# A planner that begins a pair of score tiles when its second PSUM bank is still being emptied

## The chip, the cores and the metric

The kernel runs on one core of a Trainium2 chip. The core has a matrix engine (TensorE, PE in the profile, with its weight loads shown as PEld), a ScalarE (ACT), a VectorE (DVE), a GpSimd (POOL), and a queue for transfers on SyncE (SP). PE writes into PSUM, which this kernel uses as eight banks of 128 partitions by 512 float32; the other engines read PSUM and work in SBUF. The metric is the device time of one execution in microseconds, the median of several.

## What is computed

Two layers, each made of a multi-query attention block and a mixer with an MLP, over 2048 tokens of width 512. The attention has 32 query heads of 16 elements, and all heads share one key head and one value head:

```
def _A_ref(x, wq, wk, wv, wo):              # x is the layer-normed input
    q = (x @ wq).reshape(B, S, H, Dh)...    # H = 32, Dh = 16
    k = x @ wk                              # one head for all
    v = x @ wv
    scores = einsum("bhqd,bkd->bhqk", q, k) * (Dh ** -0.5)
    p = softmax(scores)
    o = einsum("bhqk,bkd->bhqd", p, v)
    return o.reshape(B, S, H * Dh) @ wo
def _B_ref(x, w1, w2, w3, w4):
    h = gelu(layernorm(x) @ w1)             # 512 -> 512
    ...                                     # four column groups shifted by +1, -1, +2, -2 tokens
    hs = shifted @ w2
    x1 = x + hs
    return x1 + gelu(layernorm(x1) @ w3) @ w4   # 512 -> 1792 -> 512
x = x + _A_ref(layernorm(x)); x = x + _B_ref(layernorm(x))   # twice
```

The scores are 32 x 2048 x 2048 per layer, and each needs an exponential. That is the bulk of the work.

## The kernel before

**The plan.** The Python program declares operations (`Plan.op`, each with an engine, a guessed duration, a priority and the data that it reads and writes), and a list scheduler (`Plan.run`, `_pick`, `_place`) places them in simulated time, engine by engine. A lower priority number goes first. The order that comes out is written down for each engine by `emit`, with semaphore waits. So the planner's guesses decide the order; on the chip each engine then works through its own list in that order, and waits where it must. The guess for an eviction of 512 columns from PSUM by VectorE is `t_ps(512)`, 0.600 us, and 0.085 us more until the bank counts as free.

**The halves.** The attention is cut into 2,048 pieces that the code calls halves: for one chunk of queries (512 tokens, in the last two chunks of layer 1 256), one block of 4 heads, one tile of 128 keys (two for the small chunks), and one pair of heads (`p` is 0 or 1). A half is 128 x 1024 scores in two PSUM banks. Its matmuls (`qk`, line 973) contract over 32 rows, so a half uses two of the four groups of 32 rows of the matrix engine, and a half with the other `p` can run beside it.

A half is worked on in one of two ways:

- As a **unit** (`declare_unit`): two matmuls fill two of the four banks set aside for ScalarE, ScalarE takes the exponential of all 1024 columns in one instruction (line 1017, tile EA), and one group of matmuls adds the product with the values (VP) to the accumulator bank (line 1096, one half of it).
- As a **pair** (`declare_pair`): two matmuls fill two banks of a common pool, each one a tile of the pair. VectorE turns each tile into integers whose bits are an approximate bfloat16 exponential (line 1038, tile J, one instruction for each tile). GpSimd then writes two shifted copies (line 1048, tile JK), and three groups of matmuls add J and the two JK, each with its own scaled values (VD). When four of the copies are already waiting on GpSimd, a copy is planned for VectorE. There are three J buffers and four JK buffers.

Every half that goes to a pair is one that ScalarE does not have to do.

**The pool.** Banks 5, 6 and 7 are the pool. The pair tiles use them, and so does all side work: projections, transposes, output projection, mixer and MLP, each as a matmul tile that VectorE evicts. Side work has priority 10 in the main part, units 0, pair tiles 0.5, VectorE's J 1 and the product matmuls 2. When an evicting operation is placed, its bank is entered in the pool with the planned time at which it comes free. `_pick` gives a waiting tile a bank when that time plus 0.06 us (pair tiles) or 0.15 us (side work) has come. A pair tile that can't start beside a unit's score matmuls is put behind nearly everything (`deferred`, priority 11).

**When a pair begins.** Each time the score matmuls of a unit are placed, `attach` looks at the pool: with at least `FREE` = 2 banks free it calls `assign`, so that both tiles can run in the row groups that the unit leaves unused. `assign` still refuses when `MAX_PAIRS` = 2 earlier pairs are unfinished on VectorE, when the side work that is ready on VectorE comes to more than `BACKLOG` = 1 us, when a product is held back too long, or when no half with the right `p` has its data. Two stretches have stricter limits (`CALM`, `CALM_END`). If nothing was assigned for `LONELY` = 3 us, `pump` calls `assign` whatever the pool holds.

**The order of the whole.** Layer 0 has four chunks and layer 1 five. The side work of one chunk is spread (`PACE`) over the attention of the next. After the last chunk of each layer the chain output projection, mixer, MLP is urgent. At the change of layers the first chunk of layer 1 works on the keys that are there already. `filler` matmuls (ONES, NIL) fill idle time on PE to keep its clock up.

Of the kernel before, what the change touches and what calls it, by code (L numbers as in the profile page):

```python
# [15 lines left out]
class Late:  # L16
# [4 lines left out]
    def __init__(self):  # L21
        self.bank = None
        self.ops = []
        self.gates = []
# [481 lines left out]
class Kernel:  # L506
# [29 lines left out]
    FAR = 20  # L536
    FREE = 2
    LONELY = 3

    def __init__(self, nc, ins, out):  # L540
        self.nc = nc
# [651 lines left out]
    def pump(self, now):  # L1193
# [3 lines left out]
        while True:  # L1197
# [9 lines left out]
            did = True  # L1207
        if now > self.attached + self.LONELY and self.assign(now, self.ndve % 2):
            did = True
# [8 lines left out]

    def attach(self, q):

        if sum(1 for t, b in self.pl.pool if t + 0.06 <= self.pl.now) >= self.FREE:
            self.assign(self.pl.now, 1 - q.pe[3][0] // 2)

    def assign(self, now, p):
# [276 lines left out]
```

The softmax here doesn't subtract the row's maximum and nothing guards it: scores larger than these inputs give would overflow.

## Time and profile before

| | |
|---|---|
| median of 5 runs | 1599.46 us (1597.3 to 1600.16) |
| the profiled execution | 1599.78 us, of which its span is 1597.7 us |
| granted PE clock, mean | 0.998 |
| ACT busy | 1506.4 us (94%) |
| DVE busy | 1214.8 us (76%) |
| POOL busy | 1133.1 us (71%) |
| units (EA, line 1017) | 1,509 instructions, 1397.5 us |
| pair tiles (J, line 1038) | 1,078 instructions, so 539 pairs, 698.9 us |
| copies (JK, line 1048) | 955 on POOL, 123 on DVE |

The span runs from the first to the last instruction; 2.1 us lie around it. Busy shares are averages over stages that differ. The attention ends near 1540 us, and the last 58 us are the tail of the last chunk. A group of the profile's list shows the line, the engine, the operation, output and inputs, the count, then busy time, mean duration of one, and the engine's idle time just before such instructions with what ended it. Neighbouring instructions of one engine overlap a little, so busy time over count (926 ns for a unit) is less than the mean duration (1088 ns).

### The profile page before, as it was taken

To read this page: it belongs to the slowest core of one execution; us is meant where nothing else is said; L and a number is where in the kernel's file an instruction comes from. 1 tells how busy PE (TensorE), PEld (TensorE's weight loads), DVE (VectorE), ACT (ScalarE), POOL (GpSimd) and SP (SyncE) were. 2 spreads that over 40 slices of the span, in tenths; PEclk is the share of its full clock that TensorE was granted. 3 is DMA by queue.
4 is the path that set the end of the run, shared out by engine and by line. 5 is a ranking of instruction groups with operands and counts; after the bars stand their busy time and mean duration, and the time that the engine had idled before them with its cause. 6 is when DMAs were issued, how large, how long until landed. Compare 5 with 4: busy or idle time off the path is not lost.

```text
span 1597.7 us, 63318 instructions
## 1 busy us (share of the span) xinstructions
PE 1554.0 (97%) x28709; PEld 648.0 (41%) x28709; DVE 1214.8 (76%) x2145; ACT 1506.4 (94%) x1585; POOL 1133.1 (71%) x1149
## 2 busy tenths in 40 slices
PE   8999999999999999999999999999999999999999
PEld 3333333433333334343333534334433333554445
DVE  8777878877887668887785577878687876888863
ACT  4999999999999999999999779999999999999972
POOL 4799887688886557867575367787887776678640
PEclk9999999999999999999999999999999999999999
DMA  6100010001000001000000000100000000000000
GB/s 209 17 6 5 6 18 6 4 4 21 6 5 4 5 5 19 6 4 2 2 2 2 3 7 11 19 4 4 15 13 5 6 4 14 18 8 8 6 10 25
DMA packets 32142, 21.51 MB, mean 13 GB/s; under 512 B 12673, under 2 KB 31361, under 8 KB 31873
## 3 DMA queue, kind: packets, MB, share of 16 engines
q1 hardware_dynamic: 31872, 17.47, 4.6%
q8 instruction: 224, 3.67, 0.9%
q14 instruction: 46, 0.37, 0.1%
HBM read 7.90 MB, written 2.10 MB: 6 GB/s over the span
## 4 chain that ended last, share of the span: by engine, by line
ACT 74%; PE 23%; DVE 2%; issue 0%; DMA 0%; POOL 0%; SPq 0%; POOLq 0%
ACT EA L1017 69%; PE PB L625 9%; PE PB L973 7%; PE PB L1096 5%; ACT G L1428 2%; ACT L1017 1%; PE PB L791 1%; ACT GP L1348 1%; ACT L1428 1%; ACT L1348 0%; DVE G L1421 0%; DVE ST L736 0%; DVE J L1038 0%; PE PB L834 0%; PE PB L901 0%
## 5 line engine op out<-in xcount | busy, mean ns | idle before, releaser
L1017 ACT ACTIVATE EA<-PB 128x1024 bf16<-128x1024 f32 x1509 | 1397.5, 1088 | 47.3 <-PE PB L973 37.7
L1048 POOL TENSOR_SCALAR JK<-J 128x1024 uint16<-128x1024 uint16 x955 | 1009.0, 1057 | 354.9 <-DVE J L1038 228.9
L1038 DVE TENSOR_SCALAR J<-PB 128x512 uint16<-128x512 f32 x1078 | 698.9, 683 | 195.8 <-PE PB L973 191.6
L973 PE MATMUL PB<-QT,KT 32*128 32x512 bf16 (+1 forms) x4608 | 623.8, 360 | 26.0 <-ACT EA L1017 15.0
L1096 PE MATMUL PB<-EA,VP 128*32 128x256 bf16 (+1 forms) x6796 | 385.3, 264 | 0.9 <-DVE QT L1108 0.5
L973 PEld LDWEIGHTS PB<-QT,KT 32*128 32x128 bf16 x4608 | 160.4, 91 | 434.9 <-ACT EA L1017 314.1
L1096 PE MATMUL PB<-JK,VD 128*32 128x256 bf16 (+1 forms) x4840 | 288.6, 265 | 2.9 <-POOL JK L1048 1.9
L1096 PEld LDWEIGHTS PB<-EA,VP 128*32 128x32 bf16 x6796 | 159.0, 95 | 159.1 <-issue 128.5
L625 PE MATMUL PB<-ZT,W 128*32 128x512 bf16 (+2 forms) x2816 | 170.4, 342 | 0.2
L1096 PEld LDWEIGHTS PB<-JK,VD 128*32 128x32 bf16 x4840 | 114.3, 95 | 135.3 <-issue 83.7
L625 PE MATMUL PB<-ONES,NIL 128*32 128x512 bf16 x1764 | 154.3, 390 | 6.3 <-DVE ZR L773 2.0
L1096 PE MATMUL PB<-J,VD 128*32 128x256 bf16 (+1 forms) x2420 | 153.3, 263 | 1.4 <-DVE J L1038 0.6
L625 PE MATMUL PB<-W,G 128*32 128x512 bf16 x1624 | 114.4, 383 | 1.1 <-ACT G L1428 1.1
L1421 DVE CAST G<-PB 128x512 bf16<-128x512 f32 (+2 forms) x126 | 73.0, 583 | 31.7 <-PE PB L625 31.2
L1048 DVE TENSOR_SCALAR JK<-J 128x1024 uint16<-128x1024 uint16 x123 | 80.8, 664 | 4.9 <-PE PB L1096 3.6
L625 PEld LDWEIGHTS PB<-ZT,W 128*32 128x32 bf16 x2816 | 63.8, 96 | 32.5 <-issue 18.6
L1096 PEld LDWEIGHTS PB<-J,VD 128*32 128x32 bf16 x2420 | 59.8, 95 | 37.1 <-issue 22.7
L625 PEld LDWEIGHTS PB<-ONES,NIL 128*32 128x32 bf16 x1764 | 43.9, 96 | 41.9 <-issue 10.5
L1428 ACT ACTIVATE G<-G 128x3584 bf16<-128x3584 bf16 (+2 forms) x18 | 46.0, 2601 | 14.9 <-DVE G L1421 14.8
L1157 DVE TENSOR_TENSOR OS<-ACCF,PB 128x512 bf16<-128x512 bf16 (+1 forms) x72 | 44.8, 622 | 17.0 <-PE PB L1151 16.9
L756 POOL TENSOR_TENSOR SM<-SM,MH 128x4 f32<-128x4 f32 (+3 forms) x39 | 37.0, 950 | 22.4 <-DVE SM L758 19.6
L625 PEld LDWEIGHTS PB<-W,G 128*32 128x32 bf16 x1624 | 37.3, 96 | 29.7 <-issue 13.8
(94 smaller groups left out, 873.8 us busy)
## 6 DMA issues: line engine op xcount, KB each, us to landing
OT<-OS SPq DMA_DIRECT2D x424, 8.0 KB, 1.8
W<-in_B_w_dram SPq DMA_DIRECT2D x2, 1792.0 KB, 14.7
QT<-QS SPq DMA_DIRECT2D x40, 64.0 KB, 2.5
X<-in_A_x_dram SPq DMA_DIRECT2D x8, 256.0 KB, 5.1
out_dram<-OUTB SPq DMA_DIRECT2D x16, 128.0 KB, 1.7
OT<-OS SPq DMA_DIRECT2D x104, 4.0 KB, 1.8
W<-in_B_w_dram SPq DMA_DIRECT2D x2, 512.0 KB, 8.2
WQ<-in_A_wq_dram SPq DMA_DIRECT2D x1, 512.0 KB, 4.4
```

The lines of the kernel that those rows point to most:

```text
L625: ins = e.matmul(self.PB[32 * g:32 * g + 32, bank, 0:n], lhsT=lhsT[:, 32 * g:32 * g + 32], rhs=rhs, start=start, stop=stop, tile_position= ...
L756: op("POOL", lambda e: e.tensor_tensor(out=out, in0=src, in1=self.MH[:, 0, a:b], op=ALU.pow), reads=tags + [("MH",)], writes=tg(r), dur=0. ...
L791: ins = e.transpose(self.PBH[:, L.bank, j * 512 + i * 128:j * 512 + (i + 1) * 128], rows[:, tb % 4, dc * 128:(dc + 1) * 128], self.IDENT)
L973: ins = e.matmul(self.PB[:, bank, j * n:(j + 1) * n], lhsT=self.KT[32 * h:32 * h + 32, la, (kb + j) * 128:(kb + j + 1) * 128], rhs=self.QT ...
L1017: o = q.feeds = op("ACT", lambda e: e.activation(self.EA[:, ea, :, :], self.PB[:, b0:b0 + 2, :], ACTF.Exp, scale=0.25), writes=bk + [("EA" ...
L1038: o = op("DVE", lambda e, i=i, L=L: e.tensor_scalar(out=J[:, i * 512:(i + 1) * 512], in0=self.PB[:, L.bank, :], scalar1=128 * LOG2E * 0.25 ...
L1048: x = op(eng, lambda e, k=k, r=r: e.tensor_scalar(out=self.JK[:, r, :], in0=J, scalar1=float(self.STEPS[k]), scalar2=1.0, op0=ALU.add, op1 ...
L1096: ins = e.matmul(self.PB[32 * x:32 * x + 32, self.ACC, p * hw:p * hw + hw], lhsT=v[:, la, kb + j, :], rhs=ap[:, i, j * w + u * hw:j * w + ...
L1157: op("DVE", lambda e: e.tensor_tensor(out=self.OS[:, m, 0:n], in0=acc, in1=self.PB[:, M.bank, 0:n], op=ALU.mult), reads=[("ACCF", m)], wri ...
L1348: return e.activation(self.GP[:, par, :, 2:2 + n], self.GP[:, par, :, 2:2 + n], ACTF.Gelu_apprx_tanh)
L1421: op("DVE", lambda e, f=f, L=L: e.tensor_copy(self.G2[:, f, 0:n], self.PB[:, L.bank, 0:n]), writes=[L, ("G2", f)], dur=t_ps(n), give=L)
L1428: ins = e.activation(self.G2[:, a:a + 7, 0:n], self.G2[:, a:a + 7, 0:n], ACTF.Gelu_apprx_tanh)
```

## The change

A constant is added, and the test in `attach` counts a bank as available when its planned time of coming free (plus 0.06 us) lies within the next 0.45 us, not only when it is past. Nothing else is changed; the rules by which a tile gets its bank and the tests in `assign` are as they were. The order of all later work is planned anew with it.

```
@@ class Kernel
     FREE = 2
     LONELY = 3
+    SOON = 0.45
...
     def attach(self, q):
-        if sum(1 for t, b in self.pl.pool if t + 0.06 <= self.pl.now) >= self.FREE:
+        if sum(1 for t, b in self.pl.pool if t + 0.06 <= self.pl.now + self.SOON) >= self.FREE:
             self.assign(self.pl.now, 1 - q.pe[3][0] // 2)
```

More of the change, by code (lines that the diff above doesn't have):

```diff
@@ L538 @@
     LONELY = 3
+    SOON = 0.45
     def __init__(self, nc, ins, out):
@@ L1219, in attach @@
     def attach(self, q):
-        if sum(1 for t, b in self.pl.pool if t + 0.06 <= self.pl.now) >= self.FREE:
+        if sum(1 for t, b in self.pl.pool if t + 0.06 <= self.pl.now + self.SOON) >= self.FREE:
             self.assign(self.pl.now, 1 - q.pe[3][0] // 2)
```

## The prediction

> **What bounds the kernel now.** I read the page's engine sums and its chain first, then the costliest groups, then who waits for whom, then the timeline of a quiet stretch and of one with side work.
>
> ```profile
> PE 1554.0 (97%) x28709; PEld 648.0 (41%) x28709; DVE 1214.8 (76%) x2145; ACT 1506.4 (94%) x1585; POOL 1133.1 (71%) x1149
> ...
> ACT 74%; PE 23%; DVE 2%; issue 0%; DMA 0%; POOL 0%; SPq 0%; POOLq 0%
> ...
> L1017 ACT ACTIVATE EA<-PB 128x1024 bf16<-128x1024 f32 x1509 | 1397.5, 1088 | 47.3 <-PE PB L973 37.7
> L1048 POOL TENSOR_SCALAR JK<-J 128x1024 uint16<-128x1024 uint16 x955 | 1009.0, 1057 | 354.9 <-DVE J L1038 228.9
> L1038 DVE TENSOR_SCALAR J<-PB 128x512 uint16<-128x512 f32 x1078 | 698.9, 683 | 195.8 <-PE PB L973 191.6
> ...
> L1048 DVE TENSOR_SCALAR JK<-J 128x1024 uint16<-128x1024 uint16 x123 | 80.8, 664 | 4.9 <-PE PB L1096 3.6
> ```
>
> ScalarE is the bound: 74% of the chain, and before its 1,509 exponentials only 47.3 us idle. One costs 1397.5 / 1509 = 0.926 us, so a half moved from a unit to a pair is worth 0.926 us while ACT has no gaps. The takers are not full: VectorE waited 191.6 us for score matmuls ahead of a J, and POOL 228.9 us for a J.
>
> ```profile
> PEld PB L973 <- ACT EA L1017: 314.1, 895, 2.2
> ...
> POOL JK L1048 <- DVE J L1038: 228.9, 197, 8.7
> DVE J L1038 <- PE PB L973: 191.6, 241, 6.8
> ```
>
> These are waits: total, number, longest. The first says that ahead of 895 of the score groups PE stood 314.1 / 895 = 0.35 us waiting for ScalarE to empty a unit's banks. That slack covers small delays on PE.
>
> The timeline near 121 us, no side work:
>
> ```profile
> 121.04 0.39 PE L973 MATMUL PB<-QT,KT 32*128 32x512 bf16 x4
> ...
> 121.51 1.29 DVE L1038 TENSOR_SCALAR J<-PB 128x512 uint16<-128x512 f32 x2 [0.55 <-PE PB L973]
> ...
> 121.96 0.39 PE L973 MATMUL PB<-QT,KT 32*128 32x512 bf16 x2
> ...
> 122.83 0.43 DVE L1048 TENSOR_SCALAR JK<-J 128x1024 uint16<-128x1024 uint16 x1
> 122.88 0.39 PE L973 MATMUL PB<-QT,KT 32*128 32x512 bf16 x4
> ```
>
> x4 is a unit and a pair together, x2 a unit alone. Both take 0.39 us: a pair that joins a unit is free on PE. It joins every second unit, at 121.04 and 122.88, so the cadence is 1.84 us. At 121.96 two banks are being emptied: the first J of the pair began at 121.51, and of the two evictions in 1.29 us it ends near 122.16, 0.20 us after that group starts. The third bank is free. One is free and one is soon: the old test says no, the new one yes.
>
> **The change part by part.**
>
> *How often the answer changes.* For 1,336 units up to 1,365 us I rebuilt from the trace's instructions which of the three pool banks were held (a bank is held from the first matmul of its tile to the end of the eviction that reads it). At 510 units score tiles of a pair were issued too, at 826 none. Of these 826, 228 had two or more banks free already, so the other tests refused; 199 had none free; 157 had one free and no other within 0.39 us (0.45 less the 0.06 in the test); 242 had one free and another coming within 0.39 us. The change speaks to the 242: 57 of them between 50 and 200 us, where the quiet cadence rules, the others at some 8 in 50 us. Scaled to 1,509 units: 242 x 1509 / 1336 = 273. Where two banks were free, 395 of 395 + 228 units went with a pair, 63%; so some 172 pairs will be begun at a moment at which none was before. Most are not additional ones: they take the place of the pair that the next unit would have begun.
>
> *How many are additional.* That is set by the time that VectorE has left. A pair costs it two evictions of 1.29 / 2 = 0.645 us and, when POOL is full, two copies. POOL is nearly full in the quiet stretch (126 instructions busy 133.6 of 150 us between 50 and 200 us), so I charge both copies to VectorE at the mean of its 123, 0.664 us: 1.29 + 1.33 = 2.62 us. The 191.6 us of waiting would then hold 73 pairs, the upper end. I take the share of it that this test guards: of the 598 units refused for want of banks (242 + 157 + 199) the change opens 242, 40.5%. 0.405 x 191.6 / 2.62 = 30 pairs. The lower end is 0: MAX_PAIRS and the backlog test stay, and may hand the same count at other times. I take 30, since the quiet stretch, where the count of openings is thickest, shows the cover: 0.55 us of DVE waiting in each 2 x 1.84 us.
>
> *What they save.* 30 x 0.926 = 27.8 us of ScalarE. The product matmuls of a pair are three groups where a unit has one, some 0.11 us apart in the timeline: 0.22 us more PE for each half moved, 6.6 us in all, hidden beside ScalarE in the 0.35 us per group and in the fillers (154.3 us of ONES matmuls, which the planner leaves out when there is work). If that cover were gone, 6.6 us would come back.
>
> *What is late next.* The second tile of an early pair is no longer free on PE. It can join only a unit with the other pair of heads, or runs by itself. The side-work stretch near 306 us shows a group where one tile went ahead of the unit and could not share:
>
> ```profile
> 305.55 0.39 PE L973 MATMUL PB<-QT,KT 32*128 32x512 bf16 x3
> ...
> 306.10 0.60 PE L973 MATMUL PB<-QT,KT 32*128 32x512 bf16 x3
> ```
>
> 0.60 against 0.39: a lone tile costs 0.21 us. 172 x 0.21 = 36 us if all go alone and nothing hides them, 0 if all join. Behind it in PE's order stand products and the next unit's scores, and ScalarE waits for the latter; 0.21 is inside the 0.35 us of slack, so I cost it at nothing in most stretches. It has no cover where ACT is not the bound: from 800 to 960 us ACT is busy 138.5 of 160 us. I found 21 openings between 800 and 950 us, x 0.63 = 13 pairs; a side tile put off by a bank loses one eviction, 0.69 us (mean of the 512-column G evictions), at most 9 us. I take 4, half, rounded; the ends are 0 and 9. The queues of SP and POOL get nothing new: POOL's copies follow their J as before. The tail after 1540 us holds no pairs and stays, 58 us.
>
> *A rule weighed.* VectorE's copies had durations of 380 / 500 / 1402 ns (minimum, median, maximum), POOL's 1047 median; the longest is about one POOL copy, 1.05, and a free one, 0.38, end to end. The Trainium skill's page "SBUF — State Buffer", section "SBUF: two separate sides", says that VectorE in its two-port modes and GpSimd take the port pair that they share as an exclusive lock for a whole instruction. By the rule at its worst each extra copy takes 1.43 us, a pair 4.15, and the sum would be 0.405 x 191.6 / 4.15 = 19 pairs, 17 us, instead of 28; it speaks against the change, since a fuller POOL locks more often. The trace agrees with the maximum, the median says that it is mostly less.
>
> *Sum.* 1599.8 (this execution) - 27.8 + 4 = 1576. The execution lies 0.3 us above the median of 1599.46, which is nothing here. About 0.2%, 3 us, is what a measurement of this kernel can tell from no change.
>
> **The rivals.**
>
> *A, more pairs, as above: 1576.* Own range 1545 to 1594.
>
> *B, the same count, begun earlier: 1599, within 3 us.* For it: POOL at 89% between 50 and 200 us, and the 228 units at which two banks were free and nothing was begun, so banks are not the only limit. Against: 191.6 us of VectorE waiting, 228.9 us of POOL waiting.
>
> *C, slower: PE stalls in order on the second bank.* The order is written with guessed durations: an eviction 0.600 us, the trace 0.645 to 0.69; a copy on VectorE is guessed at 0.33 us and takes 0.664. A fuller VectorE runs behind the plan, and the second tile then stands at PE's head until the eviction ends, with the next unit's scores behind it. Price: up to 0.39 us of wait and 0.21 us alone, less the 0.35 of slack, 0.25 us of ScalarE's time for each of 172 pairs, 43 us; with 28 gained, +15, 1615. It decides from 28 / 172 = 0.16 us lost per early pair on. For it: between 750 and 800 us there is no filler at all, so PE has no room there. Against: in that same window ACT is busy 49.97 of 50 us, and PE now waits on a J ahead of scores only 3.5 us in the whole span. The Trainium skill's page "TensorE: Matmul & The Clock Gate", section "The mechanism" under "Part 3: Packing small matmuls — row/col tiling", says that matmuls start and end strictly in program order, which would make C's stall hit all that follows; no row here shows one overtaking.
>
> *D, all of the waiting is filled: 73 pairs, 68 us, 1532.* For it: copies took only 0.43 us in the quiet stretch. Against: only 40.5% of the bank refusals are opened.
>
> **How the numbers follow.** A 0.46, B 0.09, C 0.37, D 0.08. A is always faster, so is D; of B I count 0.07 as the same and 0.01 on each side; C is slower, up to its full price. Faster 0.55, same 0.07, slower 0.38. The range leaves out most of D below and the worst of C above: 1545 to 1617.
>
> **What would show it.** Right: about 570 pairs for 539, units near 1,480 for 1,509, VectorE's wait for scores well below 191.6 us, more groups of x3 and fewer of x2, ACT's idle before EA near 47 us. B: pairs within 5 of 539. C: pairs up or level, but ACT's idle before EA risen by tens of us with PE named as the releaser, and PE's wait ahead of L973 for a J far above 3.5 us. The prediction fails if side work, which shares the three banks, is put off so far that the stretch from 800 to 960 us or the tail grows by more than 24 us.

## The result and the profile after

| | before | after |
|---|---|---|
| median | 1599.46 us | 1595.68 us |
| ratio | | 0.9986 (95% interval 0.9981 to 0.9991) |
| the profiled execution / its span | 1599.78 / 1597.7 us | 1597.41 / 1595.6 us |
| pairs / units | 539 / 1,509 | 559 / 1,489 |
| ACT busy / idle in the span | 1506.4 / 91.3 us | 1488.2 / 107.4 us |

The kernel became faster by 0.14%: less than the 0.2% that was set as the bound of "no change", though the interval lies wholly below 1. The ratio is close to that of the means over all executions (1598.75 and 1596.47 us, 2.3 us apart); the medians are 3.8 us, 0.24%, apart. ScalarE was relieved of 18.2 us, and stood idle for 16.1 us more. That is the whole case: where did the new idle time come from?

The page of the kernel after (one line has been added above the functions, so each line number is higher by one): the engine sums, the chain, and the costliest groups.

```profile
PE 1552.6 (97%) x28725; PEld 660.2 (41%) x28725; DVE 1273.9 (80%) x2258; ACT 1488.2 (93%) x1563; POOL 1101.1 (69%) x1116
...
PE 51%; ACT 42%; DVE 6%; issue 1%; POOL 0%; DMA 0%; SPq 0%
...
L1018 ACT ACTIVATE EA<-PB 128x1024 bf16<-128x1024 f32 x1489 | 1382.1, 1069 | 46.4 <-PE PB L974 29.3
L1049 POOL TENSOR_SCALAR JK<-J 128x1024 uint16<-128x1024 uint16 x922 | 977.7, 1060 | 387.6 <-DVE J L1039 236.9
L1039 DVE TENSOR_SCALAR J<-PB 128x512 uint16<-128x512 f32 x1118 | 723.0, 682 | 156.2 <-PE PB L974 151.7
...
L1049 DVE TENSOR_SCALAR JK<-J 128x1024 uint16<-128x1024 uint16 x196 | 131.6, 678 | 12.3 <-PE PB L1097 11.1
...
L1429 ACT ACTIVATE G<-G 128x3584 bf16<-128x3584 bf16 (+2 forms) x18 | 46.0, 2601 | 31.7 <-DVE G L1422 31.6
```

Twenty more pairs, twenty units fewer, and VectorE's wait for scores is down from 191.6 to 151.7 us. The idle time ahead of the exponentials is 46.4 us, as good as the 47.3 of before. Whoever looks at that group alone finds nothing lost. The loss stands in the last line: a Gelu of the MLP, which has only 18 instructions and takes 46.0 us in both kernels, now has 31.7 us of idle time before it, where it was 14.9. The chain has changed hands too, PE leads it with 51%: a path followed back through a gap of ScalarE runs on the engine that filled the gap.

What ScalarE waits for, by line, before:

```profile
ACT EA L1017 <- PE PB L973: 37.7, 11, 18.4
ACT G L1428 <- DVE G L1421: 14.8, 1, 14.8
ACT EA L1017 <- PE PB L1096: 8.8, 3, 6.2
```

and after (total, number, longest):

```profile
ACT G L1429 <- DVE G L1422: 31.6, 2, 17.6
ACT EA L1018 <- PE PB L974: 29.3, 17, 18.6
ACT EA L1018 <- PE PB L1097: 14.9, 4, 5.6
```

The Gelu's second wait is in the tail of both kernels (14.8 and 14.0 us), the one of 17.6 is new. Gelu waits rise by 16.8 us and waits for product matmuls (L1097) by 6.1; waits for scores fall by 8.4.

To see where, I cut both executions into stages, each ended by a certain copy of the accumulator of the attention (the 32nd ends the attention of layer 0, the 47th the stretch that I call the change of layers). All columns are us, worked out from the instructions of the two traces.

| stage | length before | after | ACT idle before | after |
|---|---|---|---|---|
| attention of layer 0 | 758.1 | 739.9 | 26.6 | 24.9 |
| change of layers | 177.6 | 187.5 | 21.6 | 28.6 |
| layer 1, rest of the 512-token chunks | 419.1 | 413.6 | 0.3 | 0.8 |
| layer 1, first 256-token chunk | 91.5 | 102.4 | 0.2 | 9.7 |
| layer 1, second 256-token chunk | 92.3 | 94.0 | 0.1 | 1.4 |
| tail | 59.1 | 58.3 | 42.6 | 41.9 |

The windows view gives the same for three of these stages (window, length, busy us of PE, PEld, DVE, ACT, POOL with counts, granted clock, DMA share, GB/s). Before:

```profile
0.00:758.10 758.10, 735.06 (x12397) 288.33 (x12397) 596.96 (x1043) 731.53 (x771) 574.47 (x577) 1.00 0.08 19
758.10:935.70 177.60, 171.80 (x2920) 71.29 (x2916) 121.19 (x230) 156.05 (x160) 94.12 (x101) 1.00 0.01 2
1354.90:1446.40 91.50, 89.97 (x2566) 46.81 (x2566) 75.90 (x141) 91.35 (x97) 64.21 (x67) 1.00 0.06 13
```

After:

```profile
0.00:739.90 739.90, 719.21 (x12121) 287.80 (x12121) 619.54 (x1085) 715.00 (x758) 552.27 (x553) 1.00 0.08 19
739.90:927.40 187.50, 181.40 (x3150) 77.88 (x3146) 135.44 (x257) 158.86 (x159) 99.44 (x106) 1.00 0.01 2
1341.00:1443.40 102.40, 98.82 (x2686) 50.20 (x2682) 76.52 (x144) 92.73 (x98) 67.58 (x71) 0.98 0.06 14
```

Length less ACT busy is the idle time: 177.60 - 156.05 = 21.6 against 28.6; 91.50 - 91.35 = 0.2 against 9.7. The attention of layer 0 is 18.2 us shorter, 8.8 of them because a Gelu of the third chunk's MLP, which ran at 736 us, now runs at 790, in the next stage. Then two places give back: the change of layers 9.9 us, most of it that Gelu, and the first small chunk 10.9.

The change of layers, ScalarE's own timeline (start, length, instruction, the idle time before it). Before:

```profile
894.85 12.26 ACT L1017 ACTIVATE EA<-PB 128x1024 bf16<-128x1024 f32 x13 [6.24 <-PE PB L1096]
927.73 12.94 ACT L1017 ACTIVATE EA<-PB 128x1024 bf16<-128x1024 f32 x14 [14.73 <-PE PB L973]
```

After:

```profile
800.73 11.80 ACT L1018 ACTIVATE EA<-PB 128x1024 bf16<-128x1024 f32 x12 [1.27 <-PE PB L974]
812.55 1.28 ACT L1429 ACT_TABLE_LOAD   x1
831.47 4.78 ACT L1429 ACTIVATE G<-G 128x2688 bf16<-128x2688 bf16 x2 [17.64 <-DVE G L1422]
```

ScalarE loads the Gelu's table at 812.55 us and then waits 17.64 us, in its written order, for the G that VectorE evicts. Nothing else of its list can pass. Before, the same Gelu ran at 865.67 us without a wait, and the stage's long gaps, 14.73 and 6.24 us, stood ahead of exponentials. So the idle time ahead of EA lost one gap of this stage and gained others in the small chunk: its level sum says nothing. The attention of layer 0 ends 18.2 us earlier, but the side work that must deliver the next keys is not earlier: the evictions of the third chunk's MLP ran from 686 to 735 us before and run from 728 to 790 us after, and the keys of the eighth tile of 128 tokens, which layer 1 needs to go on, are copied at 833 us where it was 790.

The small chunk, ScalarE after:

```profile
1396.45 3.81 ACT L1018 ACTIVATE EA<-PB 128x1024 bf16<-128x1024 f32 x4
1405.83 1.94 ACT L1018 ACTIVATE EA<-PB 128x1024 bf16<-128x1024 f32 x2 [5.57 <-PE PB L1097]
```

and VectorE in its gap, with the matmuls for the OS shown (PE, line 1152):

```profile
1401.30 0.28 PE L1152 MATMUL PB<-IDENT,RZ 128*32 128x128 bf16 x8
...
1403.31 1.00 DVE L774 TENSOR_SCALAR Y<-X,MV,SM 128x512 bf16<-128x512 f32 x2 [2.76 <-POOL SM L757]
1404.23 0.41 DVE L1158 TENSOR_TENSOR OS<-ACCF,PB 128x256 bf16<-128x256 bf16 x1
...
1405.01 0.41 DVE L1129 CAST ACCF<-PB 128x256 bf16<-128x256 f32 x1
```

At the end of each block the accumulator is copied to one of two ACCF buffers, and a scaling step, which needs a pool bank for its matmuls, makes OS of it. Here the copy of a third block (at 1405.01) had to wait for the OS of the first (at 1404.23). The next block's matmuls could not go on without the accumulator, and ScalarE, which has seven EA buffers, stopped for 5.57 us. It was not a bank that held the OS: its matmuls were done at 1401.58. VectorE stood idle for 2.76 us at a Y (a layer norm of the side work) that comes earlier in its written order, until GpSimd's SM, the scale for that Y, was there.

### The profile page after: what moved, and what is told of

It is laid out like the page before. It is cut to its first block, busy times and chain, and to the rows that moved or that the text cites. A ratio compares the mean times of both kernels' runs of the same rounds, so it can differ in the third digit from the quotient of the medians.

```text
span 1595.6 us, 63539 instructions
## 1 busy us (share of the span) xinstructions
PE 1552.6 (97%) x28725; PEld 660.2 (41%) x28725; DVE 1273.9 (80%) x2258; ACT 1488.2 (93%) x1563; POOL 1101.1 (69%) x1116
## 4 chain that ended last, share of the span: by engine, by line
PE 51%; ACT 42%; DVE 6%; issue 1%; POOL 0%; DMA 0%; SPq 0%
ACT EA L1018 38%; PE PB L974 17%; PE PB L626 16%; PE PB L1097 15%; DVE J L1039 2%; ACT G L1429 2%; PE PB L792 1%; ACT L1018 1%; DVE G L1422 1%; ACT GP L1349 1%; DVE ST L737 1%; PE PB L902 0%; PE PB L1152 0%; PE PB L1137 0%; PE PB L835 0%
## 5 line engine op out<-in xcount | busy, mean ns | idle before, releaser
L1018 ACT ACTIVATE EA<-PB 128x1024 bf16<-128x1024 f32 x1489 | 1382.1, 1069 | 46.4 <-PE PB L974 29.3
L1049 POOL TENSOR_SCALAR JK<-J 128x1024 uint16<-128x1024 uint16 x922 | 977.7, 1060 | 387.6 <-DVE J L1039 236.9
L1039 DVE TENSOR_SCALAR J<-PB 128x512 uint16<-128x512 f32 x1118 | 723.0, 682 | 156.2 <-PE PB L974 151.7
L974 PE MATMUL PB<-QT,KT 32*128 32x512 bf16 (+1 forms) x4608 | 634.6, 360 | 23.8 <-ACT EA L1018 13.3
L1097 PE MATMUL PB<-EA,VP 128*32 128x256 bf16 (+1 forms) x6716 | 378.3, 264 | 2.3 <-DVE ACCF L1129 1.2
L974 PEld LDWEIGHTS PB<-QT,KT 32*128 32x128 bf16 x4608 | 164.8, 91 | 422.7 <-ACT EA L1018 285.5
L1097 PE MATMUL PB<-JK,VD 128*32 128x256 bf16 (+1 forms) x5000 | 298.6, 266 | 1.5 <-POOL JK L1049 1.2
L1097 PEld LDWEIGHTS PB<-EA,VP 128*32 128x32 bf16 x6716 | 158.9, 95 | 148.4 <-issue 118.0
L1097 PEld LDWEIGHTS PB<-JK,VD 128*32 128x32 bf16 x5000 | 118.5, 95 | 138.2 <-issue 90.0
L1097 PE MATMUL PB<-J,VD 128*32 128x256 bf16 (+1 forms) x2500 | 160.0, 265 | 1.5 <-DVE J L1039 1.0
L626 PE MATMUL PB<-ONES,NIL 128*32 128x512 bf16 x1620 | 143.7, 393 | 7.3 <-DVE ZR L774 2.1
L1049 DVE TENSOR_SCALAR JK<-J 128x1024 uint16<-128x1024 uint16 x196 | 131.6, 678 | 12.3 <-PE PB L1097 11.1
L1422 DVE CAST G<-PB 128x512 bf16<-128x512 f32 (+2 forms) x126 | 71.8, 580 | 17.6 <-PE PB L626 16.5
L1097 PEld LDWEIGHTS PB<-J,VD 128*32 128x32 bf16 x2500 | 61.9, 96 | 45.9 <-issue 30.6
L626 PEld LDWEIGHTS PB<-ZT,W 128*32 128x32 bf16 x2816 | 66.4, 96 | 29.3 <-issue 13.3
L1429 ACT ACTIVATE G<-G 128x3584 bf16<-128x3584 bf16 (+2 forms) x18 | 46.0, 2601 | 31.7 <-DVE G L1422 31.6
```

Of the source, the lines that this page charges most:

```text
L626: ins = e.matmul(self.PB[32 * g:32 * g + 32, bank, 0:n], lhsT=lhsT[:, 32 * g:32 * g + 32], rhs=rhs, start=start, stop=stop, tile_position= ...
L974: ins = e.matmul(self.PB[:, bank, j * n:(j + 1) * n], lhsT=self.KT[32 * h:32 * h + 32, la, (kb + j) * 128:(kb + j + 1) * 128], rhs=self.QT ...
L1018: o = q.feeds = op("ACT", lambda e: e.activation(self.EA[:, ea, :, :], self.PB[:, b0:b0 + 2, :], ACTF.Exp, scale=0.25), writes=bk + [("EA" ...
L1039: o = op("DVE", lambda e, i=i, L=L: e.tensor_scalar(out=J[:, i * 512:(i + 1) * 512], in0=self.PB[:, L.bank, :], scalar1=128 * LOG2E * 0.25 ...
L1049: x = op(eng, lambda e, k=k, r=r: e.tensor_scalar(out=self.JK[:, r, :], in0=J, scalar1=float(self.STEPS[k]), scalar2=1.0, op0=ALU.add, op1 ...
L1097: ins = e.matmul(self.PB[32 * x:32 * x + 32, self.ACC, p * hw:p * hw + hw], lhsT=v[:, la, kb + j, :], rhs=ap[:, i, j * w + u * hw:j * w + ...
```

## The experiments

Two theories stood against each other. One: early pairs cause both gaps, by taking pool banks from side work and from block ends. The other: the planner writes a whole new order for any edit, the gaps are an accident of the order, and so is a part of the difference between the two kernels. They are told apart by changing the order without changing the rule, and by undoing the rule in one place.

**Another order, by 5 ns.** A constant of the planner, what it adds to an operation's end before the same engine may use its result, is moved in each kernel. It is no part of the rule for pairs.

```
-    SELF = 0.035
+    SELF = 0.04
```

The kernel before with it:

> The kernel before with one planner guess moved by 5 ns (SELF 0.035 to 0.040), which gives a new order and no early pairs. Theory 1 (the early pairs cause the new ScalarE gaps): no early pairs, no new gaps; ScalarE idle in the change of layers stays near 21.6 us, in the first 256-token chunk near 0.2 us; 1596 to 1603 us. Theory 2 (any new order draws new gaps, and the order before was a lucky one): pairs stay near 539, yet gaps appear in one of the two places, 8 us or more together; 1605 to 1616 us.

The kernel after with it:

> The changed kernel with the same 5 ns. Theory 1: the gaps belong to the pairs and stay, 28.6 us in the change of layers and near 9.7 us in the first 256-token chunk; about 1596 us. Theory 2: about 560 pairs again, but the gap in the first 256-token chunk is drawn anew and may be 0; then 1586 to 1593 us, and against the first run the change is worth 15 us or more.

Measured: before with it 1608.47 us, ratio to before 1.0061 (1.0046 to 1.0076), 539 pairs as before; after with it 1594.13, ratio 0.9977 (0.9965 to 0.9989), 560 pairs, a little above the 1586 to 1593 that the second theory gave. The first small chunk without early pairs:

```profile
1349.00:1451.50 102.50, 97.32 (x2682) 49.02 (x2678) 75.12 (x139) 91.79 (x98) 65.36 (x70) 1.00 0.06 14
```

and with them:

```profile
1340.30:1437.30 97.00, 95.77 (x2692) 48.38 (x2684) 74.37 (x138) 96.74 (x100) 64.93 (x66) 1.00 0.06 15
```

The gap of the small chunk has moved: 10.7 us in the kernel that has no early pairs, 0.3 in the one that has them. It does not go with the rule: it is an accident of the order. The idle time at the change of layers has not moved: 19.5 us without early pairs, 28.4 with.

**A third buffer for the block ends**, in the kernel after.

```
-        self.OS = sb("OS", [2, 512])
+        self.OS = sb("OS", [3, 512])
-        self.ACCF = sb("ACCF", [2, 512])
-        self.RZ = sb("RZ", [2, 16])
+        self.ACCF = sb("ACCF", [3, 512])
+        self.RZ = sb("RZ", [3, 16])
-        m = self.nfin % 2
+        m = self.nfin % 3
```

> The changed kernel with three instead of two buffers for the end of a block (ACCF, RZ, OS). If the 5.6 us gap in the first 256-token chunk comes from a block whose accumulator can't be copied because the block two earlier still holds its buffer, the ScalarE idle there falls from 9.7 us to under 4 us, and with nothing else changed the time to about 1590 us. If it is PE waiting in order for banks (theory 3, my case C), the idle there stays near 9.7 us and the time near 1596.

Measured: 1597.13 us, ratio 0.9993 (0.998 to 1.0007). ScalarE's idle time in the small chunk fell from 9.7 to 2.0 us, which agrees with the reading of that gap; this run too has a new order (558 pairs), so it does not show it alone:

```profile
1340.30:1442.80 102.50, 100.91 (x2748) 50.64 (x2748) 81.45 (x152) 100.52 (x102) 64.10 (x69) 1.00 0.06 14
```

But the stage is as long as in the kernel after, because 8.8 us of other ScalarE work moved into it (13.3 us of it against 4.5), the tail took 63.0 us for 58.3, and the change of layers had 32.9 us idle. What the stage no longer lost, the new order lost elsewhere.

**No early pairs in the last chunk of layer 0**, the one before the change of layers.

```
+        at = self.halves[min(self.hi, len(self.halves) - 1)][0:2]
+        soon = 0.0 if at == (0, 3) else self.SOON
-        if sum(1 for t, b in self.pl.pool if t + 0.06 <= self.pl.now + self.SOON) >= self.FREE:
+        if sum(1 for t, b in self.pl.pool if t + 0.06 <= self.pl.now + soon) >= self.FREE:
```

> The early start switched off in the last chunk of layer 0 alone, where the side work of the third chunk is done. If the early pairs there put that side work off, and with it the keys that layer 1 can begin with, then the second group of layer 1 keys comes before 833 us again and ScalarE's idle in the change of layers falls from 28.6 us to about 22 us, at the price of 4 or 5 pairs (4 us); 1590 to 1594 us. If the gaps there come from PE stalls or from elsewhere, idle stays at 28 us or more and the lost pairs make it 1600 us.

Measured: 1592.99 us, ratio 0.9969 (0.9958 to 0.998), 554 pairs. The idle time at the change is 20.7 us, as before the change. ScalarE there:

```profile
793.14 36.72 ACT L1018 ACTIVATE EA<-PB 128x1024 bf16<-128x1024 f32 x39
829.88 1.28 ACT L1431 ACT_TABLE_LOAD   x1
833.02 4.78 ACT L1431 ACTIVATE G<-G 128x2688 bf16<-128x2688 bf16 x2 [1.86 <-DVE G L1424]
```

The attention of layer 0 ends later (745.0 us for 739.9), ScalarE has exponentials up to 829.88, and the same Gelu waits 1.86 us where it waited 17.64; the longest gap of the stage is now 7.62 us, ahead of an exponential. With five pairs fewer the kernel is faster than the one after. It is one order, and a new one, so the run agrees with the first theory at this place without settling it.

**Early pairs in one layer alone**, written against the edit above; for layer 1 alone the test is `at[0] == 1`.

```
-        soon = 0.0 if at == (0, 3) else self.SOON
+        soon = self.SOON if at[0] == 0 else 0.0
```

Layer 0 alone:

> The early start in layer 0 alone. Theory 1 with stages that add up (the stage table of before and after): -18.2 in the attention of layer 0, +9.9 in the change of layers, nothing after: about 1591 us, and no gap in the first 256-token chunk. Theory 2: the layer 0 part as above, but in layer 1 gaps drawn anew, 5 to 12 us in the 256-token chunks or the tail, without any early pair there; 1594 to 1602 us.

Layer 1 alone:

> The early start in layer 1 alone; the attention of layer 0 is planned as before to its end. Additive: the layer 1 stages of the table, -2.1 - 3.7 + 10.9 + 1.7 - 0.8 = +6: 1605 us. Theory 2: about 12 pairs more than 539 (11 us of ScalarE), but gaps in the change of layers and in a 256-token chunk that outweigh them; 1605 to 1625 us.

Measured: layer 0 alone 1599.06 us, ratio 1.0003 (0.9994 to 1.0013), 552 pairs; layer 1 alone 1617.11, ratio 1.0117 (1.0102 to 1.0132), 552 pairs. So the two halves of the change give about +1 and +19 us and together -3.8 (medians): they don't add. Layer 0 alone had gaps in layer 1's small chunks (6.7 and 3.0 us), where it began no pair early. Layer 1 alone had them there too (12.7 and 5.8), and 6.3 us in the first chunk. Each is one more drawn order, and the draw is larger than what it was to measure. The idle time at the change was 23.7 us with early pairs in layer 0 alone, 28.6 in both layers, 20.3 in layer 1 alone. With one order of each, how its rise divides stays open.

**Side work of the third chunk pulled forward**, in the kernel after, by more urgency in the planner.

```
-    URGE = ((10, 10, 10, 1.0), (10, 10, 10, 1.5, 1.0))
+    URGE = ((10, 10, 6, 1.0), (10, 10, 10, 1.5, 1.0))
```

> The changed kernel, with the side work that is done during the last chunk of layer 0 at priority 6 instead of 10 (URGE). If that side work is late because pairs go first, its W3 evictions end before 789 us and ScalarE's idle in the change of layers falls from 28.6 to about 23 us, as with the early start switched off there, but with the pairs kept; 1589 to 1594 us. If priority is not what holds it (banks are), 728 to 789 us and 28 us stay.

Measured: 1592.42 us, ratio 0.9962 (0.9947 to 0.9977), 556 pairs, idle at the change 23.0 us. The idle time went down, but not in the way expected: the evictions of that chunk's MLP ran from 718 to 787 us, at their end less than 3 us earlier than in the kernel after, and the keys were copied at 833 us as there. ScalarE still waited 15.37 us ahead of the Gelu that waited 17.64 there; the rest of the fall is in shorter gaps. Why it fell is open.

**What the draws point to.** No early pairs in the third chunk of layer 0, and the block ends of the first small chunk of layer 1 urgent.

```
-        soon = 0.0 if at == (0, 3) else self.SOON
+        soon = 0.0 if at == (0, 2) else self.SOON
...
-    RUSH = ((10, 10, 10, 1.0), (10, 10, 10, 5, 1.0))
+    RUSH = ((10, 10, 10, 1.0), (10, 10, 10, 1.0, 1.0))
```

> The early start everywhere but in the third chunk of layer 0, and the end of a block in the first 256-token chunk at priority 1 instead of 5 (RUSH). By both theories the version with the fewest gaps: idle in the change of layers near 21 us, in the first 256-token chunk near 0, about 557 pairs (18 x 0.926 = 17 us of ScalarE); 1580 to 1588 us.

Measured: 1588.99 us, ratio 0.9942 (0.9925 to 0.9958), 557 pairs: faster than both kernels, a little above what was expected.

```profile
PE 1542.6 (97%) x28621; PEld 655.2 (41%) x28621; DVE 1265.7 (80%) x2251; ACT 1492.4 (94%) x1567; POOL 1103.3 (70%) x1115
...
L1018 ACT ACTIVATE EA<-PB 128x1024 bf16<-128x1024 f32 x1491 | 1383.6, 1069 | 26.7 <-PE PB L974 24.8
```

It has two pairs fewer than the kernel after and 4.2 us more of ScalarE's work. What it has less of is idle time: 19.5 us at the change, 0.4 in the small chunk, and its span of 1587.1 us leaves 94.7 idle in all against 107.4. One order was run; how much of it is the two edits and how much the draw isn't known.

**Two more orders of each kernel**, to see what early pairs are worth apart from the draw.

```
-    SELF = 0.035
+    SELF = 0.03
```

Without and with early pairs:

> The kernel before with SELF 0.030 instead of 0.035, a third order without early pairs. Theory 2: about 539 pairs, and some gap of ScalarE that the kernel before does not have; 1600 to 1613 us. Theory 1: no new gap, 1596 to 1603 us.

> The changed kernel with SELF 0.030. Pairs again about 20 more, ScalarE busy 18 us less; idle in the change of layers 23 to 33 us, as with the early start in all of layer 0; the small-chunk gap is open. 1590 to 1605 us; against its partner, if the pairs are worth what they save less some 7 us at the change of layers, about 10 us faster.

Another constant, the time that the planner leaves before side work on PE uses a result or a freed bank, 10 ns longer (it belongs to side work, so it is a little less neutral):

```
-    MARGIN = 0.15
+    MARGIN = 0.16
```

Without and with early pairs:

> The kernel before with MARGIN 0.15 to 0.16 (side work gets a bank 10 ns later), a fourth order without early pairs. Theory 2: 530 to 540 pairs, 1599 to 1610 us. Theory 1: no new gap, 1596 to 1603 us.

> The changed kernel with MARGIN 0.16. Pairs about 20 more than its partner, idle in the change of layers 23 to 33 us, small-chunk gap open; 1592 to 1605 us, about 10 us faster than its partner if the worth of the change is the same in every order but for the draw of the gaps.

All four orders, in us (medians; ACT's busy and idle time and its idle time at the change of layers and in the first small chunk from the profiled executions; "without / with" early pairs). The ratios to the kernel before are 1.0106 (1.0091 to 1.0121) and 1.0044 (1.0029 to 1.0059) for SELF 0.03, and 1.0072 (1.0049 to 1.0096) and 1.0026 (1.0009 to 1.0043) for MARGIN 0.16; for SELF 0.03 both times lie somewhat above what was expected, and for MARGIN 0.16 the idle time at the change with early pairs, 20.6 us, lies below the 23 to 33 expected, and the difference is half of the 10 us expected.

| order | median | difference | pairs | ACT busy | ACT idle | at the change | small chunk |
|---|---|---|---|---|---|---|---|
| as given | 1599.46 / 1595.68 | -3.8 | 539 / 559 | 1506.4 / 1488.2 | 91.3 / 107.4 | 21.6 / 28.6 | 0.2 / 9.7 |
| SELF 0.04 | 1608.47 / 1594.13 | -14.3 | 539 / 560 | 1504.6 / 1485.6 | 100.4 / 110.8 | 19.5 / 28.4 | 10.7 / 0.3 |
| SELF 0.03 | 1616.00 / 1606.02 | -10.0 | 538 / 558 | 1507.8 / 1490.0 | 106.5 / 114.6 | 23.7 / 30.3 | 2.7 / 10.2 |
| MARGIN 0.16 | 1608.41 / 1603.63 | -4.8 | 531 / 556 | 1515.3 / 1494.0 | 88.1 / 108.6 | 15.1 / 20.6 | 4.3 / 4.9 |

Faster in all four, by 8.2 us (0.5%) in the mean of the medians; by the means of the executions the four are 2.3, 13.3, 9.9 and 5.5 us. Four orders that differ so much fix the sign better than the size, and in the last row single executions overlap: 1605.3 to 1614.3 us without, 1599.0 to 1608.9 with. What is the same in all four is what early pairs do: 20 to 25 more pairs, 17.8 to 21.3 us less work for ScalarE, and 5.5 to 8.9 us more idle time at the change of layers. What has either sign is the draw: the small chunk (+9.5, -10.4, +7.5, +0.6), the tail (59.1, 58.8, 63.7, 59.3 us without, 58.3, 64.2, 58.5, 63.7 with). The kernel before is a lucky draw: the three other orders without early pairs are 9 to 17 us slower. Its layer 1 makes it so: from the 47th copy to the end it takes 662.0 us, the three others 675.2, 677.2 and 670.5, and the four orders with early pairs 668.2 to 669.9. One idle time is not of the order alone: in the profiled execution of SELF 0.04 with early pairs the granted clock was 0.50 from 1224.9 to 1238.5 us, ScalarE was idle for 9.1 us in that stage (0.8 in the kernel after), and its 1598.23 us are 4.1 above the median.

## Why the prediction was wrong

**The bound and the price of a half: right.** A half moved was priced at 0.926 us; 20 x 0.926 = 18.5, and ACT's busy time fell by 18.2.

**The number of additional pairs: right in kind, too high.** 30 were predicted, 20 came. The openings were there, but fewer were used: up to 1,330 us, units with one bank free and one soon that go with a pair rose from 58 to 125, by 67, where 172 early pairs were expected. And a pair cost more than 2.62 us of VectorE: its busy time rose by 59.1, 2.96 us for each of 20. Early pairs come in bunches, find four copies waiting at GpSimd, and so send copies to VectorE: 73 more (123 to 196), of which 40 belong to the new pairs and 33 were taken from GpSimd (955 to 922). GpSimd then waited longer for a J:

```profile
PEld PB L974 <- ACT EA L1018: 285.5, 842, 2.2
...
POOL JK L1049 <- DVE J L1039: 236.9, 171, 12.9
DVE J L1039 <- PE PB L974: 151.7, 234, 2.1
```

236.9 us against 228.9. VectorE's wait gave up 39.9 us, 21% of it, not 40.5%. This term, 27.8 - 18.2 = 9.6 us, is one part of the 1597.4 - 1576 = 21.4 us by which the sum missed the profiled execution; the other, 16.1 - 4 = 12.1 us, follows below (the time outside the span fell by 0.3).

**The rule weighed: not needed.** The worst-case estimate by the lock rule of the Trainium skill's page "SBUF — State Buffer", section "SBUF: two separate sides", was 19 pairs, close to 20, but not for its reason: VectorE's copies took 393 / 561 / 1307 ns (minimum, median, maximum) beside a GpSimd that was about as busy as before (69% for 71%), mean 678 where it was 664, and not the 1.43 us that 19 rested on. A number that fits is no proof of its mechanism.

**The second tile's cost on PE: right.** PE's busy time is level (1554.0, 1552.6), although score groups of x3 rose from 139 to 211 and groups of one tile alone from 15 to 41 up to 1,330 us. PE's wait for ScalarE fell from 314.1 to 285.5 us: the slack was there, and it was used.

**What is late next: the step that failed.** The prediction found the place, 800 to 960 us, and gave it 4 us, at most 9. It worked that out from the openings inside that window and one eviction lost at each. In the traces ScalarE's whole idle time rose by 16.1 us, 7.0 of them at the change of layers and 9.5 in the first small chunk, which had no term at all. As I read it, the first was wrong in kind: a stretch in which ScalarE is not the bound doesn't lose what is put off inside it. It loses what the stage before it gains. When the attention of layer 0 ends 6 to 18 us earlier (four orders; 5 to 9 us without the 8.8 us of the Gelu that in two of them moves across that border) and the chain of side work that makes the next keys does not, the units to cover that chain are gone, and ScalarE waits longer. The idle time was larger with early pairs in each of the four orders, by 5.5 to 8.9 us, and it fell in the run that undid them in the last chunk. But the two groups overlap (15.1 to 23.7 us without, 20.6 to 30.3 with), and three of the four with early pairs have the same two later gaps in this stage, 5.24 and 3.40 us, so they are not independent orders: the link is likely, not proved. That the cause is this distance, and not another property of the order, is a reading: where some 93 us or more lay between the end of the attention of layer 0 and the copy of the eighth tile's keys (six of the kernels run here), ScalarE was idle there for 23 to 33 us; where 85 or less (the other eight), for 15 to 24; within the groups the two don't go together. ScalarE's wait ahead of the Gelu that stands at 831 us in the kernel after parts them more clearly: 15.4 to 20.3 us in the six, at most 10.4 in the eight.

The second was a thing that the prediction could not have summed: the order of the whole program is drawn anew, and a gap of 10 us falls in one stage or another.

**The sum.** The span is ScalarE's busy and idle time together: 1597.7 - 18.2 + 16.1 = 1595.6, where the prediction had -27.8 and +4.

**The rivals.** B, the same count, gave a time close to what came (1599, within 3), by a mechanism that did not happen: there are 20 pairs more. C is not it either: PE's idle time ahead of scores for a J rose from 3.9 to 9.3 us, not by tens, and the idle time ahead of EA is level. D failed with the share of the waiting; what spoke for it, copies of 0.43 us in the quiet stretch, was one copy of the timeline: the 20 between 50 and 200 us took 12.93 us, 0.65 each. The sign that was to tell C from A, the idle time ahead of EA, hid the loss, because the longest new gap stood ahead of a Gelu.

**The condition that would make it fail**, side work put off so that 800 to 960 us or the tail grows by more than 24 us, was the right one with the wrong size: the change of layers grew by 9.9 us and the tail not at all, and with 20 pairs 16.1 us more idle time, in two places, were enough.

## What to carry to other kernels

If the reading above holds, relieving the bound engine of a stage shortens the program only as far as the chain that feeds the next stage moves with it. So charge the give-back at each change of stage against what the stage before gains, and read the waits of all of the bound engine's instructions there, the rare ones above all. Where a planner writes the order, any edit draws a new one: here 5 to 10 ns in a constant moved the kernel before by 9 to 17 us, so a change worth less than about 1% has to be priced over several neutral orders of both kernels. The best single order found is worth keeping as such (1588.99 us), but it says little about the rule that came with it.

## What the runs showed of the hardware

In the profiled execution after, the granted clock of PE fell to 0.50 twice, for 3.4 us each time, where the profile of before shows 1.00 from 1425 to 1450 us:

```profile
1429.70:1433.10 3.40, 2.66 (x64) 1.31 (x61) 3.40 (x7) 3.37 (x4) 1.05 (x1) 1.00 0.03 7
1433.10:1436.50 3.40, 3.40 (x50) 1.57 (x54) 1.77 (x4) 3.37 (x3) 3.15 (x4) 0.50 0.00 0
...
1440.00:1443.40 3.40, 2.12 (x48) 0.88 (x40) 3.33 (x9) 2.04 (x3) 2.96 (x3) 0.99 0.03 5
1443.40:1446.80 3.40, 3.40 (x94) 2.15 (x94) 2.86 (x6) 2.32 (x3) 3.08 (x5) 0.50 0.02 5
```

The column before the last two is the clock. Windows of 5 us over this stretch show 0.81 to 0.85 in four of them; that is a mean of 0.50 and 1.00. In the 3.4 us ahead of each fall PE was busy for 2.66 and 2.12 us. That alone does not set the clock down: from 876.7 to 880.1 us of the same execution PE was busy for 1.64 us, and the clock stayed at 1.00 in the next 3.4 us. What does, no run here shows. ScalarE waited 2.63 us for score matmuls between the two falls (at 1440.24), a part of the 9.7 us of idle time of that chunk; whether the first fall caused it is not shown either.

The time of an execution goes with this clock: of the kernel after, the quickest took 1594.26 us at a mean granted clock of 1.000, the slowest 1603.17 us at 0.991.
